# All transposing DMAs issued from ScalarE's queue in place of SyncE's, in a fused retention and SoLU kernel

## Chip, core and metric

The kernel runs on one core of one Trainium2 chip. The metric is device time in microseconds, the median of several runs. Engines go by the short names of the profile: PE is TensorE, DVE is VectorE, ACT is ScalarE, POOL is GpSimd, SP is SyncE. A letter q behind the name (SPq, ACTq) marks what the engine's instruction queue does itself, such as issuing a DMA or waiting on a semaphore.

## What is computed

Inputs are q, k and v of shape 8 x 8 x 576 x 64 (batch, heads, sequence, head size), `moe_w_in` 512 x 1024, `moe_w_out` 1024 x 512 and `moe_g_ln` of 1024 values, all float32. The output is 4608 x 512 in float32.

```
scores = q @ k^T / 8
ret    = scores * gamma_h^(i-j) for i >= j, else 0       # causal decay per head
x      = (ret @ v), heads side by side                   # 4608 tokens x 512
h      = x @ w_in
e      = exp(h - max(h));  u = h * e / sum(e)            # SoLU
ln     = (u - mean(u)) / sqrt(var(u) + 1e-6) * g_ln
out    = ln @ w_out
```

## The kernel before

The 4608 tokens are worked as 36 chunks of 128 tokens, numbered 0 to 35. Two batch elements go side by side: chunks 0 to 7 are four blocks of 128 tokens of each, chunk 8 holds the last 64 tokens of both, and so on with every nine. Within a chunk the scores of 128 x 128 are made for eight heads, and a running state per batch element carries what earlier blocks contribute.

The program has no loops on the chip. The string `ORDER` is a list of steps `name:chunk` written out by hand; each step emits its instructions in turn, so the string sets the order of the work on every engine's queue. Buffers are rings with slots written out in `SLOTS` (`u` has 5, `uT` 5, `qkT` 4, `h` 2, the loads 6 or 7), and PSUM banks come from `BANKS`. The steps that matter here, for chunk n:

- `ld:n` loads q, k and v (L270, L274, SP). `cq`, `ck`, `cv` bring them to float16 (q and v scaled) on POOL, DVE or ACT; `ck:n` makes `k16`.
- `tq:n` (or `tr:n`) transposes `q16`, and in most chunks `k16`, on PE (L251); `eq` or `er` copies the result from PSUM to `qkT` (L243). For seven chunks, 28 to 34, `kd:n` transposes `k16` by a DMA (L326), and for chunk 34 `kq:34` does it for `q16` (L331).
- `sc:n` multiplies to scores on PE (L381), `mk:n` applies the causal mask on DVE (L394), `av:n` and `fs:n` make x^T on PE, `ex:n` copies it to `xT` (ACT mostly, L243).
- `m1:n` is x @ w_in on PE (L256, h). `mx:n` is the row maximum on DVE (L512), `xp:n` the exponential on ACT (L518), `so:n` the product u = -h * e on DVE (L527), which also frees `h`. `sq:n` sums the squares of u on ACT (L555), and `ra:n`, `rp:n` make the scale `rs` on POOL or DVE (L566, L572, L581).
- u is transposed either on PE (`tu:n`, L251, then the copy `eu:n`, L243) or by a DMA (`du:n`, L594). `du` is used for 16 chunks: 12, 14, 16, 18, 20, 22, 23, 25 and 27 to 34 (in `ORDER`, 23 stands ahead of 22 and 31 ahead of 30).
- `m2:n` is u^T @ w on PE (L256, o), `st:n` scales by `rs` on ACT (L615) and stores from SP (L621, L623). Chunk 35 is worked in halves at the end (`hm`, `hx`, `hp`, `ho`, `ht`, `he`, `hq`, `h2`, `hw`); `hw` issues its stores from SP and ACT (L729).

Where the transposing DMAs stand in `ORDER` beside ACT's steps (steps of other engines left out, `..`):

```
xp:12 .. so:12 du:12 ck:18:a er:15:a ..       xp:14 .. sq:13 so:14 du:14 .. ex:16:a
xp:16 .. so:16 du:16 .. st:14 .. ex:18:a er:19:a
ck:28:a .. du:20 kd:28 st:19 .. ex:23:a       ex:25:a .. du:23 .. ck:29:a kd:29 .. sq:22
sq:26 .. kd:34 kq:34 ex:31:v .. du:28 .. xp:29 so:29 du:29 .. st:27
```

Of the kernel before, what the change touches and what calls it, by code (L numbers as in the profile page):

```python
# [146 lines left out]
def kernel(  # L147
# [10 lines left out]
    nc = tc.nc  # L158
# [71 lines left out]
    def ring(pool, shape, dtype, name):  # L230

        at = int(next(slots[name]))
        assert at < RINGS[name]
        return pool.tile(shape, dtype, tag=f"{name}_{at}", name=name, bufs=1)
# [5 lines left out]
    T = {}  # L240
# [81 lines left out]
    def kd(n):  # L322
        if chunks[n][1] == 4 or n < BY_DMA or n in BY_PE:
            return
        T["qkT", n] = ring(att, [P, 2, 4, P], F16, "qkT")
        nc.sync.dma_start_transpose(  # L326
            out=T["qkT", n][:, 1], in_=T["k16", n].rearrange("p h d -> p (h d)")
        )

    def kq(n):  # L330
        nc.sync.dma_start_transpose(  # L331
            out=T["qkT", n][:, 0], in_=T.pop(("q16", n)).rearrange("p h d -> p (h d)")
        )

# [256 lines left out]

    def du(n):
        uT = ring(utp, [P, NF, P], F16, "uT")
        nc.sync.dma_start_transpose(out=uT, in_=T.pop(("u", n)))  # L594
        T["uT", n] = uT

    def eu(n, e="a"):
# [268 lines left out]
```

## Time and profile before

| | us |
|---|---|
| median of 3 runs | 212.85 (212.41 to 213.39) |
| profiled execution: its span, the only time that the profile gives of it | 210.9 |
| PE busy in the span | 194.3 (92%) |
| DVE busy | 181.4 (86%) |
| ACT busy | 170.5 (81%) |
| POOL busy | 157.2 (75%) |

The median of the runs is 1.9 us above the span, which holds the core's work from its first to its last instruction. In the page's 40 slices PE stands at 9 tenths or more from about 37 us to the last slices, and the granted clock is full in every slice. Nearly all DMA traffic, 47.07 of 47.71 MB, goes through the queue q1; q10 carries 0.16 MB.

In the rows shown below, a row of the timeline has start, duration, engine, line, operation and `out<-in`; rows of one kind that follow each other are merged (x2). A row of a line's view has minimum, median and maximum duration in ns, then the first and the last start. A row of the stretches has start and end, length, and busy time with number of instructions for PE, PEld, DVE, ACT and POOL, then granted clock, DMA share and GB/s.

### The profile page before, as it was taken

The numbers are of one execution on the slowest core, as the hardware profiler recorded it, in microseconds if no ns is written. First come the engines' busy times: TensorE is split into PE (matmuls) and PEld (weight loads), VectorE is DVE, ScalarE is ACT, GpSimd is POOL, SyncE is SP. The second block draws the span as 40 slices with busy tenths as digits, with TensorE's granted clock in tenths as the row PEclk, the third lists the DMA queues.
The fourth block names the chain that finished last, engine by engine and source line by source line (L and its number), as shares of the span: only waits on it lengthen the run. The fifth ranks groups of instructions, "written<-read, shape, count | busy, mean of one in ns | idle before, by whom it ended". The sixth has DMA issues, their size and how long they took to land.

```text
span 210.9 us, 7583 instructions
## 1 busy us (share of the span) xinstructions
PE 194.3 (92%) x3125; PEld 124.0 (59%) x3125; DVE 181.4 (86%) x323; ACT 170.5 (81%) x299; POOL 157.2 (75%) x226
## 2 busy tenths in 40 slices
PE   0887798999999999999999999999999998999992
PEld 0464476575666657657566667575656654565562
DVE  0486999979997999899989999999879998999760
ACT  2424999898979999999898978999679976677981
POOL 5377899676689899888839798879999977545620
PEclk9999999999999999999999999999999999999999
DMA  5999998999898989999999899999989999899754
GB/s 134 257 330 294 258 272 290 253 209 299 224 215 258 265 215 273 221 251 230 208 275 197 205 231 238 273 226 206 179 143 256 210 166 205 156 247 199 154 174 149
DMA packets 110834, 47.71 MB, mean 226 GB/s; under 512 B 94536, under 2 KB 104784, under 8 KB 110800
## 3 DMA queue, kind: packets, MB, share of 16 engines
q1 hardware_dynamic: 110480, 47.07, 99.7%
q8 instruction: 24, 0.39, 0.8%
q10 hardware_dynamic: 320, 0.16, 0.3%
q14 instruction: 10, 0.08, 0.2%
HBM read 32.54 MB, written 9.44 MB: 199 GB/s over the span
## 4 chain that ended last, share of the span: by engine, by line
PE 55%; SPq 14%; DMA 8%; DVE 8%; POOL 7%; ACT 3%; issue 3%; DVEq 0%; POOLq 0%
PE o L256 21%; PE h L256 18%; SPq L274 5%; SPq L270 5%; DMA w_out<-in_moe_w_out_dram 3%; PE tp L251 3%; PE sc L381 3%; PE lp L251 3%; DMA qkT<-k 2%; PE x L456 2%; POOL v L279 2%; SPq L789 2%; DMA qf<-in_q_dram 2%; PE x L256 2%; SPq L779 2%
## 5 line engine op out<-in xcount | busy, mean ns | idle before, releaser
L256 PE MATMUL h<-w_in,xT 128*64 128x512 f16 x560 | 66.9, 380 | 0.1
L256 PE MATMUL o<-w_c,uT 128*64 128x512 f16 x480 | 56.9, 380 | 0.0
L394 DVE TENSOR_TENSOR ret<-sc,tris 128x512 f16<-128x512 f32 x72 | 46.1, 682 | 2.8 <-PE sc L381 2.5
L256 PEld LDWEIGHTS <-xT 128*64 128x64 f16 x576 | 31.5, 110 | 23.1 <-issue 0.7
L512 DVE TENSOR_REDUCE nm<-h 128x1 f32<-128x1024 f32 x35 | 42.6, 1216 | 2.8 <-PE h L256 2.7
L256 PEld LDWEIGHTS <-uT 128*64 128x64 f16 x560 | 31.0, 110 | 23.0 <-issue 0.6
L527 DVE SCALAR_TENSOR_TENSOR u<-h,e 128x1024 f16<-128x1024 f32 x35 | 42.5, 1215 | 1.5 <-ACT e L518 1.4
L518 ACT ACTIVATE e<-h,nm 128x1024 f32<-128x1024 f32 x35 | 39.4, 1125 | 5.0 <-DVE nm L512 3.1
L432 POOL TENSOR_TENSOR s<-t,small 128x512 f16<-128x512 f32 x32 | 33.9, 1063 | 7.4 <-DVE t L420 6.1
L555 ACT ACTIVATE sq<-u,su 128x1024 bf16<-128x1024 f16 x30 | 34.8, 1159 | 2.0 <-DVE u L527 2.0
L581 POOL TENSOR_TENSOR rs<-w,mhalf 128x1 f32<-128x1 f32 x36 | 20.3, 570 | 20.7 <-DVE w L572 17.2
L290 POOL TENSOR_TENSOR q<-qf,small 128x512 f16<-128x512 f32 x30 | 31.2, 1043 | 5.4 <-DMA qf<-in_q_dram 5.1
L279 POOL TENSOR_TENSOR v<-vf,small 128x512 f16<-128x512 f32 x30 | 31.7, 1062 | 2.8 <-DMA vf<-in_v_dram 2.5
L615 ACT ACTIVATE o_sb<-o,rs 128x512 f32<-128x512 f32 x35 | 24.0, 692 | 4.5 <-POOL rs L581 3.2
L243 ACT COPY qkT<-tp 128x512 f16<-128x512 f16 x42 | 23.0, 599 | 5.0 <-PE tp L251 4.9
L243 ACT CAST xT<-x 128x512 f16<-128x512 f32 x29 | 17.1, 593 | 3.1 <-PE x L256 2.8
L251 PE MATMUL tp<-ident,q 128*64 128x128 f16 x232 | 12.4, 230 | 6.0 <-POOL q L290 5.5
L243 ACT CAST k<-kf 128x512 f16<-128x512 f32 x17 | 10.5, 626 | 7.7 <-DMA kf<-in_k_dram 7.7
L456 PE MATMUL x<-ret,v 128*64 128x128 f16 x288 | 14.8, 222 | 2.1 <-DVE ret L394 1.5
L251 PEld LDWEIGHTS <-q 128*64 128x64 f16 x280 | 11.0, 115 | 8.9 <-POOL q L290 5.7
L381 PE MATMUL sc<-qkT 64*128 64x128 f16 x288 | 14.7, 223 | 1.3 <-DMA qkT<-k 0.8
L444 POOL TENSOR_TENSOR s<-t,small 128x256 f32<-128x256 f32 x24 | 15.3, 638 | 0.9 <-DVE t L420 0.8
(87 smaller groups left out, 272.1 us busy)
## 6 DMA issues: line engine op xcount, KB each, us to landing
qf<-in_q_dram SPq DMA_DIRECT2D x36, 256.0 KB, 5.1
kf<-in_k_dram SPq DMA_DIRECT2D x36, 256.0 KB, 5.0
vf<-in_v_dram SPq DMA_DIRECT2D x36, 256.0 KB, 5.5
out_dram<-o_sb SPq DMA_DIRECT2D x35, 256.0 KB, 4.2
w_in<-in_moe_w_in_dram SPq DMA_DIRECT2D x4, 512.0 KB, 6.0
w_out<-in_moe_w_out_dram SPq DMA_DIRECT2D x4, 512.0 KB, 6.5
uT<-u SPq DMA_TRANSPOSE x16, 4.6
out_dram<-o_sbh SPq DMA_DIRECT2D x2, 64.0 KB, 1.8
```

The lines of the kernel that those rows point to most:

```text
L243: (engine.copy if engine is nc.scalar else engine.tensor_copy)(out=out, in_=in_)
L251: nc.tensor.transpose(out=out[w], in_=in_[:, w], identity=ident)
L256: nc.tensor.matmul(out=out[w], lhsT=lhsT[:, w], rhs=rhs, start=start, stop=stop, skip_group_check=True,)
L279: engine.tensor_tensor(out=dst, in0=T.pop((key, n)), in1=table.unsqueeze(2).to_broadcast([P, H, D]), op=ALU.mult,)
L290: ENG[e].tensor_tensor(out=dst.rearrange("p (a h) d -> p h a d", h=2), in0=T.pop(("qf", n)).rearrange("p (h a) d -> p h a d", h=2), in1=ta ...
L394: nc.vector.tensor_tensor(out=r, in0=s, in1=m, op=ALU.mult)
L432: nc.gpsimd.tensor_tensor(out=s16, in0=t.unsqueeze(2).to_broadcast([P, 4, 2, D]), in1=gd.unsqueeze(3).to_broadcast([P, 4, 2, D]), op=ALU.mult,
L512: nc.vector.tensor_reduce(out=nm, in_=T["h", n], axis=AX.X, op=ALU.max, negate=True)
L518: nc.scalar.activation(out=e, in_=T["h", n], func=ACT.Exp, bias=T.pop(("nm", n)), accum_out=s)
L527: nc.vector.scalar_tensor_tensor(out=u, in0=T.pop(("h", n)), scalar=-1.0, in1=T.pop(("e", n)), op0=ALU.mult, op1=ALU.mult, accum_out=su,)
L555: nc.scalar.activation(out=s, in_=T.pop(("v", n)), func=ACT.Square, scale=-float(DFF), bias=T.pop(("su", n)), accum_out=ss,)
L615: nc.scalar.activation(out=o_sb, in_=T.pop(("o", n)), func=ACT.Copy, scale=T.pop(("rs", n)))
```

## The change

The three places that issue a transposing DMA call it on `nc.scalar` in place of `nc.sync`. The instructions stand where they stood in `ORDER`; they now lie in ACT's instruction queue between ACT's own steps. Loads and stores stay where they are.

```diff
     def kd(n):
...
-        nc.sync.dma_start_transpose(
+        nc.scalar.dma_start_transpose(
             out=T["qkT", n][:, 1], in_=T["k16", n].rearrange("p h d -> p (h d)")
         )

     def kq(n):
-        nc.sync.dma_start_transpose(
+        nc.scalar.dma_start_transpose(
             out=T["qkT", n][:, 0], in_=T.pop(("q16", n)).rearrange("p h d -> p (h d)")
         )
...
     def du(n):
         uT = ring(utp, [P, NF, P], F16, "uT")
-        nc.sync.dma_start_transpose(out=uT, in_=T.pop(("u", n)))
+        nc.scalar.dma_start_transpose(out=uT, in_=T.pop(("u", n)))
         T["uT", n] = uT
```

## Prediction

> **What bounds the kernel now.** I read the page first, then the busy time by stretch, then the rows of the moved instructions, then what ACT does just before and after each.
>
> ```profile
> span 210.9 us, 7583 instructions
> PE 194.3 (92%) x3125; PEld 124.0 (59%) x3125; DVE 181.4 (86%) x323; ACT 170.5 (81%) x299; POOL 157.2 (75%) x226
> ...
> uT<-u SPq DMA_TRANSPOSE x16, 4.6
> ...
> qkT<-k SPq DMA_TRANSPOSE x7, 3.0
> ...
> qkT<-q SPq DMA_TRANSPOSE x1, 4.4
> ```
>
> PE is busy 92% of the span, and 24 transposes are issued by SP. The first is issued at 95.4 us, so only the time after about 88 us can change. I cut it into five stretches (columns: PE, PEld, DVE, ACT, POOL):
>
> ```profile
> 88.00:104.00 16.00, 15.81 (x280) 10.23 (x272) 15.60 (x25) 14.79 (x28) 12.64 (x20) 1.00 1.06 232
> 104.00:135.00 31.00, 30.71 (x528) 19.87 (x528) 29.19 (x49) 27.13 (x48) 24.83 (x35) 1.00 1.08 231
> 135.00:155.00 20.00, 19.54 (x352) 12.78 (x350) 19.25 (x34) 16.41 (x30) 17.16 (x25) 1.00 1.08 207
> 155.00:176.00 21.00, 20.70 (x342) 13.18 (x338) 19.15 (x31) 17.92 (x32) 18.04 (x27) 1.00 1.05 196
> 176.00:207.00 31.00, 30.18 (x392) 17.58 (x386) 24.85 (x53) 25.01 (x46) 15.71 (x27) 1.00 0.93 188
> ```
>
> PE is the bound here, with about 2% idle: whatever holds it up, it can't win back. DVE is close behind. ACT is idle 1.2, 3.9, 3.6, 3.1 and 6.0 us, 17.7 us in all. That is the whole room for what the change puts on ACT's queue.
>
> **The price of an issue.**
>
> ```profile
> L594 SPq DMA_TRANSPOSE uT<-u x16: 1238/1440/3667, 95.4 to 198.2; - x16
> ...
> L326 SPq DMA_TRANSPOSE qkT<-k x7: 1195/1224/2036, 143.0 to 176.9; - x7
> ...
> 178.18 1.26 SPq L331 DMA_TRANSPOSE qkT<-q  x1
> ...
> 206.81 1.45 ACTq L729 DMA_DIRECT2D out_dram<-o_sbh  x2
> ...
> 206.81 1.39 SPq L729 DMA_DIRECT2D out_dram<-o_sbh  x2
> ```
>
> A transpose holds SP's queue for at least 1.20 to 1.24 us; what is over that stands beside a full DMA queue or waits of SP. No row shows one on ACT. The nearest are the stores of L729, issued by both engines at once: 1.45 us for two on ACT, 1.39 on SP. So I take SP's undisturbed price, 1.24 us. Below it the nearest row is ACT's own store, 0.7 us; above it SP's median, 1.44. These are the ends; 24 issues are 29.8 us, or 17 to 35 between them. The room is 17.7.
>
> **How much of it stops ACT.** ACT's queue can work ahead of its engine:
>
> ```profile
> L615 ACTq EVENT_SEMAPHORE  x1: 1718/1718/1718, 81.1 to 81.1; - x1
> ...
> 81.07:82.79 1.72, 1.72 (x20) 0.80 (x18) 1.72 (x5) 1.72 (x5) 1.72 (x3) 1.00 1.06 324
> ```
>
> A semaphore wait of 1.72 us ahead of a store's scaling ran in the queue while ACT was busy for all of these 1.72 us with earlier instructions. So an issue whose data are ready can hide behind one or two instructions that already wait at the engine. It cannot hide where DVE has yet to make u, since the queue then waits with nothing more handed on. Chunk 16 is the pattern:
>
> ```profile
> 109.33 1.14 ACT L518 ACTIVATE e<-h,nm 128x1024 f32<-128x1024 f32 x1
> ...
> 110.43 0.71 ACT L615 ACTIVATE o_sb<-o,rs 128x512 f32<-128x512 f32 x1
> ...
> 111.46 1.13 ACT L243 COPY qkT<-tp 128x512 f16<-128x512 f16 x2
> ...
> 110.90 1.22 DVE L527 SCALAR_TENSOR_TENSOR u<-h,e 128x1024 f16<-128x1024 f32 x1
> 112.04 0.08 DVE L527 DVE_READ_ACCUMULATOR u<-h,e 128x1 f32 x1
> ...
> 113.35 0.40 PE L381 MATMUL sc<-qkT 64*128 64x128 f16 x8
> ```
>
> `du:16` stands between `xp:16`, the exponential at 109.33, and `st:14`, the scaling at 110.43. DVE makes u from that exponential until 112.12. The queue waits for it, issues for 1.24 us, and `st:14` starts at 113.36: 2.92 us late. Behind it stand `ex:18` and the copies of `er:19`, which end at 112.59 and now at 115.5. PE's scores of chunk 19, at 113.35, wait 2.2 us for them. That is where the loss reaches the engine that sets the end.
>
> Eleven of the 24 are of this kind (12, 14, 16, 18, 23, 25, 27, 29, 31, 33, 34). The late start of ACT's next instruction is the end of u plus 1.24 less its recorded start. First and last:
>
> ```profile
> 90.92 0.61 ACT L243 CAST k<-kf 128x512 f16<-128x512 f32 x1
> ...
> 93.34 0.08 DVE L527 DVE_READ_ACCUMULATOR u<-h,e 128x1 f32 x1
> ...
> 198.04 0.08 DVE L527 DVE_READ_ACCUMULATOR u<-h,e 128x1 f32 x1
> 198.07 1.26 ACT L615 ACTIVATE o_sb<-o,rs 128x512 f32<-128x512 f32 x2
> ...
> 198.19 1.24 SPq L594 DMA_TRANSPOSE uT<-u  x1
> ```
>
> Chunk 12: 93.42 + 1.24 - 90.92 = 3.7. Chunk 34: 198.12 + 1.24 - 198.07 = 1.3. The eleven in order of chunk: 3.7, 2.3, 2.9, 1.9, 1.4, 2.5, 1.9, 3.6, 2.6, 3.4, 1.3, together 27.5 us.
>
> For keys, `kd:28` and `kd:29` stand right behind ACT's own cast of `k16`, and the queue waits for that cast to end:
>
> ```profile
> 136.31 1.12 ACT L243 CAST k<-kf 128x512 f16<-128x512 f32 x2
> 137.34 0.69 ACT L615 ACTIVATE o_sb<-o,rs 128x512 f32<-128x512 f32 x1
> ...
> 176.51 1.15 ACT L555 ACTIVATE sq<-u,su 128x1024 bf16<-128x1024 f16 x1
> ...
> 176.93 1.20 SPq L326 DMA_TRANSPOSE qkT<-k  x1
> ...
> 178.11 1.11 ACT L518 ACTIVATE e<-h,nm 128x1024 f32<-128x1024 f32 x1 [0.36 <-DVE nm L512]
> ```
>
> `kd:28`: the cast ends at 137.43, plus 1.2, so `st:19` starts 1.3 late; I take the same for `kd:29`: 2.6 us. Then `kd:34`, `kq:34` and `du:28` stand in a row ahead of `xp:29`. Their data are there by 176.93, when SP began; three issues end at 180.6, where `xp:29` started at 178.11: 2.5 us. The other eight (`du` of 20, 22, 30, 32, `kd` of 30 to 33) have data that are ready or nearly so, and work ahead of them at the engine. I take 0.2 us each, 1.6 in all; if nothing hid them they would be 10.
>
> The sum on ACT is 27.5 + 2.6 + 2.5 + 1.6 = 34.2 us against 17.7 us of idle time. Chained as they are, not all idle time gives way. By stretch, added less what I let the idle time give back:
> - 88 to 104: 6.0 added (12, 14), 1.2 idle, 4.8 left.
> - 104 to 135: 4.8 added (16, 18), 3.9 idle; following ACT and PE as above, PE is 2.2 late after the first and about 3 after both: 3.0 left.
> - 135 to 155: 4.4 added; most of the 3.6 idle is two waits for POOL's `rs` (3.2 below), which these issues do not move: 1.4 left.
> - 155 to 176: 5.0 added, half of it given back by waits for PE: 2.5 left.
> - 176 to 207: 14.0 added, of which the waits for DVE's row maximum (`nm`) and others give back 5: 9.0 left.
>
> Together 20.7 us.
>
> **What SP gains.** SP loses 24 issues, 33 us of its queue by the medians. Behind them loads and stores come sooner, and a key's transpose no longer waits behind loads. What that can be worth is what PE, POOL and ACT lose to it now:
>
> ```profile
> ACT o_sb L615 <- POOL rs L581: 3.2, 2, 1.9
> ACT e L518 <- DVE nm L512: 3.1, 7, 0.9
> ...
> PE sc L381 <- DMA qkT<-k: 0.8, 1, 0.8
> ...
> POOL q L279 <- DMA qf<-in_q_dram: 2.6, 1, 2.6
> ...
> POOL q L290 <- DMA qf<-in_q_dram: 1.5, 1, 1.5
> ```
>
> PE waited 0.8 us for a transposed key, which goes. POOL's 4.1 us waiting for q come as DMA engines are already busy (share 1.05 to 1.08), and POOL has idle time; I count 0. So 20.7 - 0.8 = 19.9 us: 210.9 becomes 230.8, and with the 1.9 us between span and median, 212.85 becomes about **233 us**.
>
> **Two rules of the Trainium skill against these rows.** An issue takes 1.24 us and the data of `uT` land 4.6 us after it, so the issue is a quarter of the transfer and as long as an exponential on ACT. The Trainium skill, "DMA: Bandwidth & Descriptors", section "Issuing engines are not separate DMA queues", says that issuing from several engines only saves issue time, usually small beside the DMA; by it the sum would be near 0, and the trace does not bear it out for this queue.
>
> That a DMA's wait stops what follows on ACT is read from the program order, and no row shows it on ACT. The Trainium skill, "Perfetto Trace Analysis", section "Per-engine timelines", says that a compute instruction waits in a queue of its own while the sequencer goes on, but a DMA's semaphore wait is the sequencer's. The 1.72 us row agrees with the sequencer being ahead. If a DMA's wait, too, let later work pass, the eleven would cost 1.24 each, 13.6 in place of 27.5, and the total would be near 223.
>
> **The rivals.**
> - **The issue hides after all.** If ACT's stops are short (u comes sooner once DVE has less in front of it) and ACT's idle time takes nearly all: 34.2 less some 9 us of shorter waits less 17.7 gives 7 to 8, about 220. For it: ACT has that idle time. Against: PE is 2.2 us late after the first stop of its stretch.
> - **Dearer issues.** If SP's long issues (up to 3.67 us) go with the transpose and not with SP's place in the queue, or the eight do not hide, 8 to 15 us more come: 243 to 253. For it: the DMA engines stay full. Against: the key's issues are 1.22 at the median under the same load.
> - **Faster, by SP's relief.** PE's 0.8 us and POOL's 4.1 us go, and the queue's running ahead covers all the issues: 208 to 212, say 209. It decides if ACT's added idle time ahead of the instructions behind the 24 issues stays below some 5 us, 0.2 us each. For it: data for eight of the 24 are there early. Against: the eleven that wait for DVE by construction, with 1.2 us of u between exponential and issue.
> - **Issue time is negligible.** Then neither sum counts, and the time stays at 213.
>
> **How the numbers follow.** Forecast (225 to 243): 0.66. Hidden for the most part (214 to 225): 0.13. Dearer (243 to 256): 0.15. Faster: 0.04. No change: 0.02. Since 0.5%, about 1 us, is what a measurement of this kernel can tell from no change, that is 0.04 faster, 0.02 same, 0.94 slower. A range from 221 to 248 takes in the forecast's own, some 5 points of the lighter case and 8 of the dearer: 8 in 10.
>
> **What would show it.** In the profile after: 24 rows DMA_TRANSPOSE on ACTq, 1.2 to 1.4 us each; ACT with some 30 to 35 us of idle time after 88 us, most of it ahead of the instructions behind `du` (the casts, copies and scalings named); ACT busy unchanged at 170; PE's idle time up by about 20 us, ended by ACT's `qkT`, `xT` and by DVE's `ret` behind them; PE's 0.8 us wait for `qkT<-k` gone. Wrong it would be if the issues on ACT were far from 1.24 us, if instructions behind a `du` started before u was made, or if PE stayed at 98% in the stretches.

## The result and the profile after

The kernel with the change takes **241.92 us** (median of 4 runs, 239.34 to 245.65), the kernel before on the same chip 212.63 us (211.27 to 213.39): the ratio is 1.136, with an interval of 1.127 to 1.145. The forecast was 233 us, with a range of 221 to 248: the sign was right, and the number 9 us too low. The profiled execution, the fastest of the four, took 239.34 us; its span is 237.6 us, 26.7 us more than before. Here and below a median is over all runs, while a ratio and its interval leave out runs that are more than 1.5% above the fastest of the same kernel.

The page of the kernel after: span and busy times, the granted clock in 40 slices, two queues, and the landing of `uT`.

```profile
span 237.6 us, 7581 instructions
...
PE 202.0 (85%) x3125; PEld 130.5 (55%) x3125; DVE 181.8 (77%) x323; ACT 171.2 (72%) x299; POOL 157.6 (66%) x226
...
PEclk9999999999999999799999799999999999599998
...
q10 hardware_dynamic: 21568, 5.41, 13.8%
...
uT<-u ACTq DMA_TRANSPOSE x16, 3.1
```

ACT is busy for as long as before (171.2 us, 170.5 before) and so are DVE and POOL: none of them got more to do, and what is added on ACT is waiting. PE's busy time did grow, by 7.7 us, for the same 3125 instructions. The transposes have moved to queue q10 (5.41 MB, 0.16 before), and `uT` lands 3.1 us after the issue in place of 4.6, a gain on which nothing waited. New is the line PEclk: three slices below 8 tenths.

The rows of the moved issues after, by line (minimum, median, maximum in ns):

```profile
L594 ACTq DMA_TRANSPOSE uT<-u x16: 1248/1250/1921, 93.2 to 223.5; - x16
...
L326 ACTq DMA_TRANSPOSE qkT<-k x7: 1204/1206/1342, 149.0 to 193.9; - x7
```

ACT's sequencer pays at the median what SP's did when nothing disturbed it, 1.21 to 1.25 us. The timeline after shows ACT behind the issue of chunk 12, at chunk 16, at `kd:28`, at the row `kd:34`, `kq:34`, `du:28`, and at chunk 34; DVE and PE at chunk 16 (in brackets the idle time ahead of an instruction, and the releaser that the view infers):

```profile
94.59 0.62 ACT L243 CAST k<-kf 128x512 f16<-128x512 f32 x1 [3.86 <-issue]
...
101.61 0.58 ACT L243 CAST xT<-x 128x512 f16<-128x512 f32 x1 [1.60 <-PE x L256]
...
114.87 1.16 ACT L518 ACTIVATE e<-h,nm 128x1024 f32<-128x1024 f32 x1
...
116.43 1.21 DVE L527 SCALAR_TENSOR_TENSOR u<-h,e 128x1024 f16<-128x1024 f32 x1
117.57 0.08 DVE L527 DVE_READ_ACCUMULATOR u<-h,e 128x1 f32 x1
117.68 1.39 ACTq L594 DMA_TRANSPOSE uT<-u  x1
119.19 0.69 ACT L615 ACTIVATE o_sb<-o,rs 128x512 f32<-128x512 f32 x1 [3.07 <-POOL v L279]
119.93 0.32 PE L405 MATMUL kp<-v,k 128*64 128x64 f16 x8 [1.54 <-ACT o_sb L615]
121.38 0.40 PE L381 MATMUL sc<-qkT 64*128 64x128 f16 x8 [0.34 <-ACT qkT L243]
...
137.71 1.07 ACT L243 COPY qkT<-tp 128x512 f16<-128x512 f16 x2 [2.72 <-PE tp L251]
...
150.47 0.69 ACT L615 ACTIVATE o_sb<-o,rs 128x512 f32<-128x512 f32 x1 [1.47 <-POOL s L444]
...
193.88 1.22 ACTq L326 DMA_TRANSPOSE qkT<-k  x1
195.13 1.29 ACTq L331 DMA_TRANSPOSE qkT<-q  x1
196.74 1.92 ACTq L594 DMA_TRANSPOSE uT<-u  x1
198.71 1.11 ACT L518 ACTIVATE e<-h,nm 128x1024 f32<-128x1024 f32 x1 [3.19 <-issue]
...
225.31 1.27 ACT L615 ACTIVATE o_sb<-o,rs 128x512 f32<-128x512 f32 x2 [1.37 <-POOL rs L581]
```

Chunk 16 is read thus: the exponential begins at 114.87, DVE makes u until 117.65, the issue begins 0.03 us later, and the scaling `st:14`, which stood ready behind it, begins 0.12 us after the issue ends. ACT stood still for 3.07 us, and PE's `kp` waited 1.54 us for that scaling. The bracket names POOL as releaser of `st:14`; the row of the issue just above shows what it really was. Releasers are inferred, and an issue on the engine's own queue often appears under another name.

The waits after, from 88 us on (total, times, longest), show where PE and DVE pay:

```profile
DVE ret L394 <- PE sc L381: 10.8, 7, 3.7
...
PE sc L381 <- ACT o_sb L615: 7.3, 4, 3.6
...
PE sc L381 <- ACT qkT L243: 3.8, 2, 3.5
```

PE waits for ACT's scalings and copies, and DVE for PE behind them. Last the stretches (start and end, length; busy time of PE, PEld, DVE, ACT, POOL; granted clock, DMA share, GB/s). Of the kernel before, from 88 us to its end:

```profile
88.00:210.90 122.90, 117.03 (x1872) 73.64 (x1864) 108.53 (x189) 101.27 (x183) 88.37 (x130) 1.00 1.01 207
```

Of the kernel after, the same stretch, and below it steps of 3.4 us, one after the other in pairs:

```profile
88.00:237.60 149.60, 124.57 (x1858) 79.83 (x1854) 109.30 (x189) 101.80 (x182) 88.24 (x130) 0.95 0.75 168
...
92.95:96.36 3.41, 0.12 (x4) 0.13 (x6) 0.19 (x2) 1.77 (x4) 3.12 (x6) 1.00 1.18 237
96.36:99.78 3.42, 3.42 (x36) 2.01 (x34) 2.43 (x4) 3.42 (x6) 0.00 (x0) 0.50 1.07 163
...
130.49:133.91 3.42, 1.74 (x32) 1.17 (x30) 2.07 (x3) 2.59 (x5) 3.42 (x4) 1.00 0.44 87
133.91:137.32 3.41, 3.41 (x30) 1.59 (x28) 2.64 (x4) 1.08 (x2) 3.12 (x4) 0.50 0.60 165
...
174.87:178.29 3.42, 1.84 (x33) 1.46 (x34) 1.31 (x3) 2.42 (x5) 3.42 (x5) 1.00 1.22 239
178.29:181.70 3.41, 3.41 (x50) 2.09 (x46) 3.41 (x6) 3.41 (x6) 0.86 (x4) 1.00 0.43 136
```

The books from 88 us on: ACT busy 101.8 us against 101.3, so its idle time grew by all of the 26.7 us but 0.5. PE's idle time went from 5.9 to 25.0 us (+19.1), and its busy time from 117.0 to 124.6 (+7.5) for the same work. Most of the last is the clock: in the four steps at half speed (from 96.4, 133.9, 202.2 and 205.6) PE was busy for 11.4 us, so some 5.7 of the 7.5 us are theirs by estimate; the rest is open. The clock is granted in steps of 3.41 us. In this trace a step in which PE stood idle for 1.68 us or more in sum is followed by one at half speed; after 1.58 us of idle time it stayed full (178.3).

### The profile page after: what moved, and what is told of

It is laid out like the page before. It is cut to its first block, busy times and chain, and to the rows that moved or that the text cites. A ratio compares the mean times of both kernels' runs of the same rounds, so it can differ in the third digit from the quotient of the medians.

```text
span 237.6 us, 7581 instructions
## 1 busy us (share of the span) xinstructions
PE 202.0 (85%) x3125; PEld 130.5 (55%) x3125; DVE 181.8 (77%) x323; ACT 171.2 (72%) x299; POOL 157.6 (66%) x226
## 3 DMA queue, kind: packets, MB, share of 16 engines
q10 hardware_dynamic: 21568, 5.41, 13.8%
## 4 chain that ended last, share of the span: by engine, by line
PE 34%; ACT 14%; DVE 14%; POOL 11%; issue 8%; DMA 7%; SPq 6%; ACTq 4%; POOLq 0%; DVEq 0%
PE o L256 14%; PE h L256 10%; DVE nm L512 3%; DMA w_in<-in_moe_w_in_dram 3%; DVE u L527 3%; ACT e L518 3%; DMA w_out<-in_moe_w_out_dram 3%; ACT o_sb L615 3%; POOL q L290 3%; ACTq L594 2%; PE tp L251 2%; ACT sq L555 2%; POOL v L279 2%; ACT qkT L243 2%; SPq L274 2%
## 5 line engine op out<-in xcount | busy, mean ns | idle before, releaser
L256 PE MATMUL h<-w_in,xT 128*64 128x512 f16 x560 | 69.7, 391 | 0.1
L256 PE MATMUL o<-w_c,uT 128*64 128x512 f16 x480 | 58.2, 385 | 3.6 <-ACT o_sb L615 2.3
L256 PEld LDWEIGHTS <-uT 128*64 128x64 f16 x560 | 32.8, 111 | 26.1 <-issue 5.3
L256 PEld LDWEIGHTS <-xT 128*64 128x64 f16 x576 | 33.5, 113 | 23.8 <-issue 3.1
L581 POOL TENSOR_TENSOR rs<-w,mhalf 128x1 f32<-128x1 f32 x36 | 20.4, 570 | 27.2 <-DVE w L572 23.8
L290 POOL TENSOR_TENSOR q<-qf,small 128x512 f16<-128x512 f32 x30 | 31.9, 1063 | 4.2 <-DMA qf<-in_q_dram 4.1
L381 PE MATMUL sc<-qkT 64*128 64x128 f16 x288 | 16.1, 229 | 13.8 <-ACT o_sb L615 7.3
L381 PEld LDWEIGHTS <-qkT 64*128 64x128 f16 x288 | 9.3, 98 | 23.2 <-issue 13.6
L243 ACT CAST k<-kf 128x512 f16<-128x512 f32 x17 | 10.6, 630 | 12.5 <-DMA kf<-in_k_dram 7.2
L456 PE MATMUL x<-ret,v 128*64 128x128 f16 x288 | 15.5, 227 | 3.1 <-DVE ret L394 2.0
L251 PE MATMUL tp<-ident,q 128*64 128x128 f16 x232 | 12.9, 236 | 5.7 <-POOL q L290 5.4
L444 POOL TENSOR_TENSOR s<-t,small 128x256 f32<-128x256 f32 x24 | 14.6, 612 | 3.3 <-DVE t L420 2.6
```

The lines of the kernel that those rows point to most:

```text
L243: (engine.copy if engine is nc.scalar else engine.tensor_copy)(out=out, in_=in_)
L256: nc.tensor.matmul(out=out[w], lhsT=lhsT[:, w], rhs=rhs, start=start, stop=stop, skip_group_check=True,)
L290: ENG[e].tensor_tensor(out=dst.rearrange("p (a h) d -> p h a d", h=2), in0=T.pop(("qf", n)).rearrange("p (h a) d -> p h a d", h=2), in1=ta ...
L381: nc.tensor.matmul(out=s[e][:, hp], lhsT=qkT[dd, 1, hp], rhs=qkT[dd, 0, hp], start=True, stop=True,)
```

## The experiments

The theory is the forecast's: an issue on ACT's queue waits in order until u is made, holds the queue for 1.25 us more, and ACT's later work, then PE, is late by that sum. Against it stand that the issues cost by their number alone, that the wait alone costs, and that the lower clock makes a large part of it.

**One issue alone (only12).** The kernel before, with chunk 12's transpose on ACT:

```diff
-        nc.sync.dma_start_transpose(out=uT, in_=T.pop(("u", n)))
+        q = nc.scalar if n == 12 else nc.sync
+        q.dma_start_transpose(out=uT, in_=T.pop(("u", n)))
```

> The kernel before, with the transpose of u of chunk 12 alone issued by ACT; the other 23 stay on SP. Theory (ACT's queue stops until u is made, PE then idles, and a long idle of PE is followed by a stretch at a lower granted clock): the cast behind the issue starts some 4 us later, PE idles 3 to 3.5 us ahead of the scores of chunk 15, the clock is granted at half for about 3.4 us after it, and since PE can't make up for it the time rises by 3.5 to 5.5 us, to 216 to 218. Rival, the issue time alone counts: 1.2 us more, 214. Rival, one stop is made up downstream: less than 1 us more.

Measured: 219.50 us, ratio 1.032 (1.021 to 1.044); in a second, longer comparison (only12_again, five rounds) the ratio was 1.023 (1.014 to 1.032). One issue in 24 costs some 5 to 7 us, so they don't cost by number. In the first profile the stop was larger than the 3.9 us of the kernel after:

```profile
91.81 0.53 SPq L274 DMA_DIRECT2D vf<-in_v_dram  x1
...
94.20 0.08 DVE L527 DVE_READ_ACCUMULATOR u<-h,e 128x1 f32 x1
...
96.67 1.40 ACTq L595 DMA_TRANSPOSE uT<-u  x1
98.11 0.62 ACT L243 CAST k<-kf 128x512 f16<-128x512 f32 x1 [6.23 <-issue]
...
105.92 0.59 ACT L243 CAST xT<-x 128x512 f16<-128x512 f32 x1 [2.31 <-PE x L256]
```

u was made at 94.28, but the issue began at 96.67. The wait ahead of it was one for the completion semaphore that SP's load of v, issued at 91.81, also uses: in the trace eight such semaphores go in turn to the DMAs of both queues, and that load landed 4.8 us after its issue, at 96.60. The wait has a row of its own on ACT's queue, and it ends at 96.64:

```profile
L595 ACTq EVENT_SEMAPHORE  x1: 17/17/17, 96.6 to 96.6; - x1
```

The same wait made the issue of chunk 12 begin later than its u in first4 (by 0.3 us), only12_fill_again (0.5) and filler (1.1). In the kernel after it ended before u was made, and each of the eleven issues there began 0.03 us after its u. The tie was not tried apart. In the steps of the clock the same kernel shows two long idle times of PE (3.41 and 1.75 us), each with a step at half speed behind it:

```profile
94.60:98.01 3.41, 0.00 (x0) 0.00 (x0) 0.00 (x0) 0.00 (x0) 2.62 (x5) 1.00 1.22 259
98.01:101.42 3.41, 1.66 (x26) 1.38 (x28) 1.02 (x2) 3.30 (x7) 0.00 (x0) 0.50 1.13 230
101.42:104.84 3.42, 3.42 (x24) 1.56 (x20) 1.41 (x3) 2.19 (x4) 0.81 (x2) 0.50 1.21 253
```

**Four issues (first4).** The same line with `n < 20`: chunks 12, 14, 16 and 18.

> The transposes of u of chunks 12, 14, 16 and 18 issued by ACT, the other 20 by SP. Theory: the four stops (4.0, 1.7, 3.2 and 2.0 us in the profile after) are passed on nearly whole, as nothing later has room: 9 to 12 us more than before, 222 to 225, and ACT as late at chunk 20 as in the kernel after (11 to 12 us). Rival, ACT's idle time gives most of it back once the stops end: under 6 us more. Rival, the loss comes from the key's transposes and the last chunks: near 213.

Measured: 225.82 us, ratio 1.064 (1.047 to 1.080). The four stops are 4.2, 1.6, 2.9 and 2.0 us, as in the kernel after. ACT was 13.5 us late at chunk 20 and 12.0 at the end: of the loss that stands there (1.4 us of it from before the first issue, see the table below), the whole idle time of the last 100 us gives back only 1.5. That speaks against the step of the forecast by which each stretch's idle time takes a part of the stops.

**The wait without the issue (wait_only).** SP issues as before; ACT instead copies eight columns of u, which makes it wait for u at the same place:

```diff
-        nc.sync.dma_start_transpose(out=uT, in_=T.pop(("u", n)))
+        u = T.pop(("u", n))
+        nc.sync.dma_start_transpose(out=uT, in_=u)
+        look = tiny.tile([P, 8], F16, name="look")
+        nc.scalar.copy(out=look, in_=u[:, DFF - 8 :])
```

> The kernel before, all transposes issued by SP, but at the place of each of the 16 transposes of u ACT copies the last 8 columns of u to a tile that nothing reads. So ACT waits for u where the changed kernel does, and issues nothing. Theory (the wait for u in ACT's order is one half of the loss, the issue of 1.25 us behind it the other): the stops at the eleven late ones fall from about 28 to about 15 us, time 8 to 15 us above before, 221 to 228. Rival, the issue time is what counts: under 4 us above before. Rival, the wait is everything: as after, 238 or more.

Measured: 218.62 us, ratio 1.030 (1.023 to 1.037), +6.3 us and below the 8 to 15 that the theory gave. ACT's wait, and the copies' own time (total of busy time, mean ns, then idle time):

```profile
ACT look L597 <- DVE u L527: 12.0, 9, 2.4
```

```profile
L597 ACT COPY look<-u 128x8 f16<-128x8 f16 x16 | 3.1, 195 | 12.1 <-DVE u L527 12.0
```

15.1 us were put in and 5.8 us of span came out. Small stops are taken up; the wait in the program order is real, but alone it gives less than a quarter of the change's 26.7 us.

**Twice the issues (halves).** The kernel after, each `du` as two transposes of half the size, the same bytes:

```diff
-        nc.scalar.dma_start_transpose(out=uT, in_=T.pop(("u", n)))
+        u = T.pop(("u", n))
+        for i in range(2):
+            nc.scalar.dma_start_transpose(
+                out=uT[:, 4 * i : 4 * i + 4], in_=u[:, 512 * i : 512 * i + 512])
```

> The kernel after, with each of the 16 transposes of u issued by ACT as two, of 512 columns each: the same waits, the same bytes, 16 issues more of about 1.2 us, 19 us on ACT. Theory (each issue behind a wait stops ACT for its whole length): 12 to 18 us above the kernel after, 254 to 260. Rival, the wait for u alone counts and issues hide: within 4 us of after, 238 to 246.

Measured: 262.22 us, ratio 1.236 (1.229 to 1.244), 20.3 us more than the kernel after.

```profile
L596 ACTq DMA_TRANSPOSE uT<-u x32: 1204/1288/2538, 93.9 to 245.9; - x32
```

An issue of half the bytes takes as long (1.29 us at the median): its price does not go with the size. 16 more at 1.29 are 20.6 us, and 20.3 came: once the idle time is used up, an issue on ACT counts in full. (The profile also has nine steps at half speed behind 88 us, against four in the kernel after; what they add was not taken apart.)

**Issues later in ACT's order (later).** All 24 on ACT, but the issues of eleven `du`, of `kd:28`, `kd:29`, `kd:34` and `kq:34` moved behind more of ACT's work, so that their data are made by then (`du:28` moved forward). For a moved chunk `du` only takes the buffer, and a new step, `di`, issues (`ki` and `kj` for keys and q):

```diff
- xp:12 .. so:12 du:12 ck:18:a er:15:a ..
+ xp:12 .. so:12 du:12 ck:18:a er:15:a .. er:16:a di:12 sq:12
- xp:16 .. so:16 du:16 .. st:14 .. ex:18:a er:19:a
+ xp:16 .. so:16 du:16 .. st:14 .. ex:18:a er:19:a .. di:16 er:20:a
...
```

> The kernel after, all 24 issues on ACT, with 11 of the transposes of u, the key's of chunks 28, 29 and 34 and that of q moved in ACT's program order: behind so many of ACT's steps that by the profile of before the data are ready and the issue done before ACT's next step is due (28 moved ahead, as its u is ready early). Theory (the wait for u in ACT's queue is most of the loss, 24 issues of 1.24 us by themselves can hide behind work at the engine): ACT's stops behind the issues fall from 34 us to under 10, time 213 to 222. Rival, the issue time itself can't be hidden on ACT, 30 us against 18 us of idle time: 230 or more.

Measured: 221.98 us, ratio 1.046 (1.036 to 1.056). The same 24 issues on the same queue cost some 10 us in place of 29. The place in the order thus makes two thirds of the change's cost. What is left is a missed expectation: the stops were to fall below 10 us and came to 17.7.

```profile
L607 ACTq DMA_TRANSPOSE uT<-u x16: 1247/1266/2662, 96.4 to 208.1; - x16
```

```profile
114.27 1.13 ACT L244 COPY qkT<-tp 128x512 f16<-128x512 f16 x2
114.83 1.41 ACTq L607 DMA_TRANSPOSE uT<-u  x1
116.28 1.07 ACT L244 COPY qkT<-tp 128x512 f16<-128x512 f16 x2 [0.88 <-DVE t L426]
```

This issue is in part hidden: it begins 0.57 us before the copies ahead of it end, and ACT is idle for 0.88 us in place of 1.4. A few others lasted up to 2.66 us; why is open.

**Does the clock make the rest (filler, only12_fill)?** Small matmuls of no use, put on PE where it stands still, keep it busy. First in the kernel after, at three places (in the scores of chunks 15, 21 and 34):

```diff
+        for _ in range({15: 12, 21: 6, 34: 12}.get(n, 0)):
+            nc.tensor.matmul(out=s[0], lhsT=ones, rhs=w_out16[:, 0], start=True, stop=True)
```

> The kernel after, with 12, 6 and 12 matmuls of no use put on PE ahead of the scores of chunks 15, 21 and 34, where PE idled 3.5, 1.3 and 3.6 us and the granted clock fell afterwards. Their results are overwritten by the scores. Theory that the clock adds to the stops: granted clock back to 0.98 or more of full, PE idle less by what the fillers take, time 4 to 7 us below the kernel after, 235 to 238. Rival, the slower clock lies in the shadow of ACT's stops: same time as after, 240 to 242. Rival, fillers only add work to PE: 3 to 6 us above after.

Measured: 245.16 us, ratio 1.156 (1.142 to 1.171), 3.2 us above the kernel after, as the reading had it by which fillers only add work; the two intervals just overlap. The mean clock was 0.962 in the profiled run and 0.976 to 0.979 in the other three (0.950 to 0.969 in the kernel after), so it rose a little at most, and no time came of it. The run missed its aim: the fillers at chunk 15 left 1.9 us of idle time, and a half step followed still; the first ones at chunks 21 and 34 began only after PE had been idle for 1.3 and 3.4 us, held up as the scores were. So it decides nothing on the clock. The cleaner pair is one stop alone, with 20 fillers in chunk 15:

> The transpose of u of chunk 12 alone on ACT, and 20 matmuls of no use (about 4.3 us) on PE ahead of the scores of chunk 15, in the idle time of 5.9 us that stood there in the run without them. Theory (PE's idle time of about 1.7 us or more in a stretch of 3.4 us brings the half clock in the next): no stretch at half clock after the stop, and the time 1.5 to 3.5 us below the run without the fillers, 216 to 218. Rival, the clock's cost is hidden behind ACT: the same time as without them, 219.5. Rival, the fillers themselves delay the scores: above 220.

```profile
94.03 1.88 ACTq L597 DMA_TRANSPOSE uT<-u  x1
95.95 0.62 ACT L243 CAST k<-kf 128x512 f16<-128x512 f32 x1 [4.36 <-issue]
...
101.72 0.58 ACT L243 CAST xT<-x 128x512 f16<-128x512 f32 x1 [0.39 <-PE x L256]
```

```profile
93.35:96.80 3.45, 3.45 (x20) 1.49 (x17) 0.65 (x2) 0.85 (x2) 3.45 (x7) 1.00 1.18 278
96.80:100.20 3.40, 3.40 (x44) 1.88 (x44) 1.80 (x3) 3.40 (x8) 0.14 (x1) 1.00 1.20 174
```

Kept busy, PE keeps the full clock behind a stop as long, and ACT's next wait for PE is 0.39 us, near the 0.43 of the kernel before, and not the 1.48 to 2.31 us of the kernels with a half step there. The times: 216.85 us, ratio 1.023 (1.017 to 1.030). The first only12 had a longer stop, so the pair was run once more, five rounds each:

> The transpose of u of chunk 12 alone on ACT once more, beside the same with the matmuls of no use on the same chip. Theory (the half clock after PE's long idle time adds to the stop): 218.5 to 220, one or two stretches of 3.4 us at half clock after about 96 us, and 1.5 to 3 us above the kernel with the matmuls. Rival (the slower clock lies in the shadow of ACT): the same time as that one within 1 us.

> The same with 20 matmuls of no use on PE ahead of the scores of chunk 15. Theory: the clock stays full and the time is 216 to 217.5, 1.5 to 3 us below the one without. Rival: within 1 us of it.

Measured: 219.52 (ratio 1.0226, 1.0135 to 1.0317) without fillers, and 217.73 (1.0229, 1.0164 to 1.0295) with. The ratios rest on two runs without fillers (216.20 and 217.75) and four with (216.13 to 218.25); the two kernels can't be told apart. The profile of only12_again still shows the half step behind its stop of 3.95 us:

```profile
93.35:96.76 3.41, 0.00 (x0) 0.00 (x0) 0.26 (x2) 1.60 (x4) 3.19 (x6) 1.00 1.13 265
96.76:100.17 3.41, 3.37 (x34) 2.09 (x36) 2.43 (x4) 3.39 (x6) 0.00 (x0) 0.50 1.09 186
```

Between the instruction behind the issue and `sq:13`, some 9 us on, the lateness grew from 4.2 to 5.4 us here, from 3.7 to 4.9 in the kernel after, and from 7.2 to 9.2 where two half steps followed (only12); with fillers it stayed at 5.0. So a half step costs about 1.2 us on the spot. At the next `sq`, 0.7 us of that was gone again (4.7 here, 8.5 in only12), while with fillers nothing changed (5.1). From there to the end all three lost another 1.2 to 1.5 us of lateness, and what one half step is worth in the total is below what the times can tell, about 1%.

Stops that ACT was given, and what the span gained:

| kernel | stops, us | span, us more than 210.9 | of this, late at `xp:12` already, us |
|---|---|---|---|
| wait_only | 12.1, and 3.1 of copies | 5.8 | 0.6 |
| only12_again | 4.0 | 3.6 | 0.2 |
| only12, first profile | 6.2 | 7.1 | 0.9 |
| first4 | 10.7 | 12.1 | 1.4 |
| later | 17.7 | 10.6 | 1.3 |
| after | 33.7 | 26.7 | -0.3 |
| filler | 38.6 | 35.1 | 2.7 |
| halves | 53.1 | 48.6 | 0.4 |

The last column is the start of `xp:12` less its start before, 89.81: it stands ahead of the first moved issue, so it is no effect of the change, and it has to be taken off. Then small stops spread over the whole run (wait_only, later) lose 8 to 10 us on the way; from there on each us counts (later to after: 16.0 more, 17.7 more of span; after to halves: 19.4 and 21.2). A few long stops early on lose nothing (only12 and first4) or little (only12_again: 0.6).

## Why the prediction was right, and where it fell short

**The price of an issue** was right: 1.24 us taken, 1.21 to 1.25 measured at the median (single ones up to 1.92). The ends, 0.7 and 1.44, were not needed.

**That an issue waits in order for u** was right. Each of the eleven began 0.03 us after its u was made, also where ACT's work stood ready behind it. The Trainium skill, "Perfetto Trace Analysis", section "Per-engine timelines", has it so (a DMA's wait is the sequencer's), and chunk 16 agrees: u at 117.65, issue at 117.68. By the other reading the eleven would have cost 13.6 us; they cost 25.7.

**The stops** were right nearly one by one: 33.7 us against 34.2. That the totals lie so close is in part luck: the eleven came out 1.8 us lower than forecast, and the others 1.3 higher. The eleven, forecast 27.5, measured 25.7 (3.9, 1.6, 3.1, 1.9, 1.4, 2.3, 1.9, 2.7, 2.6, 3.0 for chunk 33 with 32, and 1.4). `kd:28` and `kd:29`: 2.6, measured 2.8. The row ahead of `xp:29`: 2.5, measured 3.2. The eight that were to hide: 1.6, measured 2.0. The queue does run ahead of ACT, where the data are there.

**What the idle time gives back** was the step that failed: of 34.2 us it was to take 13.5, and it took about 7. The lateness of ACT's instructions against the sums by stretch:

| behind | before, us | after, us | late | forecast |
|---|---|---|---|---|
| `du:12` | 90.92 | 94.59 | 3.7 | 3.7 |
| `du:16` (`st:14`) | 110.43 | 119.19 | 8.8 | 7.7 |
| `kd:28` (`st:19`) | 137.34 | 150.47 | 13.1 | 9.1 |
| `du:28` (`xp:29`) | 178.11 | 198.71 | 20.6 | 14.2 |
| `du:34` (`st:26`) | 198.07 | 225.31 | 27.2 | 20.7 |

The first stop is right to a tenth, and the last stretch adds 6.6 where 6.5 were forecast; the 6.5 us that are missing arise between 94 and 199 us, in the middle stretches, from which the forecast had taken 1.8, 3.0 and 2.5. The most arises early: at 135 us of the kernel before, ACT was 11.6 us late, where 7.8 were forecast and the four stops up to there sum to 10.5, so on balance idle time had given nothing back. Between 94 and 178 us of the kernel before, ACT's idle time was 6.6 us of waits for PE's `x`, `tp` and `tr` and 3.2 for POOL's `rs`, among others. In the kernel after the waits for `rs` shrank to 0.6, about as forecast; those for PE still came to 6.2. That they stay because PE's work is itself chained to ACT, and moves with it, fits this but was not tried apart. A part has a cause that was in no term of the sum: the clock. Behind the two half steps, ACT waits for PE 1.60 us at 101.61 and 2.72 at 137.71, where the kernel before waits so (the timeline of before):

```profile
96.72 0.58 ACT L243 CAST xT<-x 128x512 f16<-128x512 f32 x1 [0.43 <-PE x L256]
...
126.16 1.07 ACT L243 COPY qkT<-tp 128x512 f16<-128x512 f16 x2 [0.90 <-PE tp L251]
```

That is 1.2 and 1.8 us more, 3.0 of the 6.5 at most. It is a reading of one trace: the pair with and without fillers shows the local effect, and there 0.7 of 1.2 us was soon gone again. How the 6.5 divide between the clock and the waits that moved along stays open. The two half steps from 202.2 on lie in the last stretch, which came out as forecast.

**PE idle up by about 20, ACT busy unchanged** were right (19.1; 171.2 against 170.5), as was **what SP's relief brings**: the wait of 0.8 us for `qkT<-k` is gone, POOL's 4.1 us for q shrank to 0.6, and no time came of it.

**The rivals.** Hiding for the most part, faster, and no change fell with the stops of 33.7 us. Dearer issues did not come true either: the price was the one forecast. The time alone would not have ruled them out, for the sum of that rival is off: 8 to 15 us more than 233 are 241 to 248, not 243 to 253, and 241.9 lies in that range. Of the 9 us that were missing, 6.8 are in the span (237.6 against 230.8); the rest is that the median lies 4.3 us above the profiled span, where 1.9 were taken.

## What to carry over

A DMA that is issued from a compute engine's queue costs that engine its issue time and, if its data aren't made yet, the wait for them too: put it behind several us of work that is already queued (here that cut the cost from 29 to 10 us, not to nothing), or leave it to an engine with nothing behind it. Sum such stops one by one from the trace; here their total came out within 2%, and the eleven large ones within 7%. Don't take an engine's idle time as room for them before it is seen what that idle time waits for: where it waits for work that seems chained to the engine itself, it can move along (6.6 us of waits for PE were still 6.2 here).

## What was not expected of the hardware

- **The clock falls early.** Counted over all eleven profiles from 20 us on, in steps of 3.41 us that themselves ran at full speed: up to 1.58 us of idle PE in sum was never followed by half speed, 2.06 us and more always was, and in between it went both ways (half after 1.68, 1.69, 1.82 and 1.89; full after 1.68, 1.72, 1.76, 1.90 and 2.01). A step already at half speed needed less: after 1.10 us (halves) and 1.38 us (filler) the next was at half speed too. The Trainium skill, "TensorE: Matmul & The Clock Gate", section "Why this matters for your kernels", advises against gaps over about 3 us and speaks of one window of idling; its section "Part 1: The HAM clock gate" gives that window as 3413 ns. The length of the step agrees (3.41 us here), the gap does not: less was enough, and here the measurement decides.
- **A transpose's issue costs the same for half the bytes**: 1.29 us at the median for 512 columns, 1.25 for 1024.
- **Queues are tied by their completion semaphores**: a transpose on ACT began 2.4 us after its data were ready, 0.07 us after a load on SP's queue landed.
